# Fixed operand places, earlier weight sums and a port rule in the planner of an attention and feed-forward kernel

## The chip, the cores and the metric

The kernel runs on one core of one Trainium2 chip. The metric is the device time of one execution in microseconds (us).

## What is computed

An attention layer over 4 batches, 8 heads, 576 positions and head size 64, whose scores get a bias from a small network on relative positions, followed by a gated feed-forward layer over the 2304 tokens:

```
scores = q @ k.T / 8 + bias            # bias: relu(x * w1 + b1) @ w2 over |i - j|
attn   = softmax(scores) @ v           # 4 x 8 heads, 576 x 576 scores each
x      = attn as [2304, 512]
h      = x @ w_in                      # [2304, 2048]
out    = (h * sigmoid(h)) @ w_out      # [2304, 512]
```

The inputs of the feed-forward layer arrive as 64-bit floats and are narrowed to 32 bits on the chip.

## The kernel before, in words

**Precision.** Each f32 operand of a large matmul is kept as a rounded high half and a low half (the remainder); a product is three matmuls (high by high, high by low, low by high; `PAIRS`). The high half is a copy (line 274 on VectorE, line 272 on ScalarE), the low half a subtraction (line 277, on VectorE or GpSimd).

**Order.** No engine's order is written out by hand. `Plan` is a list scheduler that runs on the host. Each operation has a kind, a cost for every engine that may do it, a due time and the buffers it reads and writes (`op`, lines 67 to 91). `order` (lines 118 to 212) plays the program through with these costs, with a delay (`LAG`) after each, and gives each free engine the ready operation with the smallest due time; for an operation that another engine could do too, engines other than GpSimd add a penalty. What comes out is a fixed order of instructions on each engine. On the chip the engines then wait for data alone: no instruction waits because of a planned time. `take` hands out places in SBUF and PSUM: a tag has a fixed number of places (`caps`; 27 of tag `G`, 12 of `M`, 2 of `pt`, 2 of `w`), and a buffer keeps its place from its first operation until its last. All DMAs go through one queue (SP), in the planned order, so a load or store that waits holds up all behind it.

**Stages.** The attention of batch 0 with the making of the bias comes first. Then batches 1 and 2, and batch 3, go on beside two plain feed-forward blocks of 384 tokens (`ff_block`, 16 steps each). Block 0 also narrows all weights: four VectorE operations in a row on each of 32 tiles (`narrow`, lines 360 to 377), then a split into halves (`split`); the 16 tiles of `w_out` then stay in `G` until the end, those of `w_in` are stored to HBM (line 851). Block 1 loads them again (line 856). By then attention is done, and three super blocks of 512 tokens follow (`ff_super`, 8 steps each), which do the first product of the layer with seven instead of eight sub-products: operands are 256 columns of x or sums of them (`super_x`: line 686 multiplies by the softmax factor, line 694 forms the sums, then 14 pairs of halves), weights are tiles of `w_in` or sums and differences of two of them (`sums_of`: lines 723 and 728, then `split`, then a store to `ts_d` at line 732). A step has 42 matmuls of 256 columns (line 747) and 24 of 512 columns for the second product (line 804).

**Where the weight sums are made.** In block 2, the first super block, each step loads two tiles of `w_in` and calls `sums_of` for them; blocks 3 and 4 load the stored sums (line 840).

**Where the operands lie.** Each call of `super_x` asks for two new buffers of `pt` and four of `M`. The first ten pairs of halves are laid in `pt` in turn, the last four in `M`. In the plan a product reads whole buffers (line 742), so it follows every half that is written to the two `pt` buffers, and a new block's buffers can be had only when the last product of the block before that reads them is done:

```
pts = [buf("pt", [128, 5, 2, 256], F32R) for _ in range(2)]     # 676
...
dst, at = pts[n % 2], n // 2                                    # 698
...
@op("p_mm", ("PE", 0.71), t0 + 0.8 * k, reads=[w, xs[name, 0][0], xs[name, 1][0]], writes=[dst])   # 742
```

The `pt` buffers are also what attention keeps its transposed probabilities in (line 476).

Of the kernel before, what the change touches and what calls it, by code (L numbers as in the profile page):

```python
# [9 lines left out]
F32R = mybir.dt.float32r  # L10
# [36 lines left out]
class Plan:  # L47
# [11 lines left out]
    LAG = {"PE": 0.2, "ACT": 0.15, "DVE": 0.13, "POOL": 0.15, "SP": 0.95}  # L59
# [58 lines left out]
    def order(self):  # L118
# [13 lines left out]
        num, dma, mode = 0, 0.0, 0  # L132
# [13 lines left out]
        while events:  # L146
# [17 lines left out]
            for e in sorted(free, key=lambda e: free[e]):  # L164
# [8 lines left out]
                while wait[e]:  # L173
# [42 lines left out]
def attention_moe_kernel(ctx: ExitStack, tc: tile.TileContext, q, k, v, small, w_in, w_out, lut, ident_d, out):  # L216
# [96 lines left out]
    def bias_tile(st, t0):  # L313
# [8 lines left out]
        for ig in range(4):  # L322
            @op("bias_f", {"ACT": 0.22 + n * 0.00086, "DVE": 0.15 + n * 0.0009} if ig or st % 2 == 0 or st < 4 else {"POOL": 0.12 + n * 0.0045},
# [15 lines left out]
        @op("bias_ev", {"ACT": 0.29 + BW * 0.00083, "DVE": 0.26 + BW * 0.00103}, t0 + 2.5, reads=[bps, cb], writes=[bsb])  # L339
# [11 lines left out]
    def narrow(t0, w, src):  # L351
# [4 lines left out]
        @op("abs", ("ACT", 0.67), t0, reads=[d], writes=[w])  # L356
# [3 lines left out]
        @op("clamp", ("DVE", 0.5), t0 + 0.1, writes=[w])  # L360
# [3 lines left out]
        @op("shift", ("DVE", 0.56), t0 + 0.2, writes=[w])  # L364
# [4 lines left out]
        @op("low", ("DVE", 0.9), t0 + 0.3, reads=[d], writes=[w])  # L369
# [4 lines left out]
        @op("sign", ("DVE", 0.8), t0 + 0.4, reads=[d], writes=[w])  # L374
# [4 lines left out]
    def split(t0, w):  # L379
# [3 lines left out]
        @op("split_hi", ("ACT", 0.62), t0 + 0.5, reads=[w], writes=[(wr, 0)])  # L383
# [3 lines left out]
        @op("split_lo", {"POOL": 1.36, "DVE": 0.9}, t0 + 1, reads=[w, (wr, 0)], writes=[(wr, 1)])  # L387
# [23 lines left out]
    def keys(b, hp, t0):  # L411
# [4 lines left out]
        @op("k_hi", {"ACT": 1.16, "DVE": 0.85}, t0 - 8, reads=[kst], writes=[khi])  # L416
# [3 lines left out]
        for a in range(2):  # L420
            @op("k_lo", {"POOL": 1.55, "DVE": 0.95}, t0 - 6 + 0.1 * a, reads=[kst, khi], writes=[(klo, a)])
# [10 lines left out]
    def queries(b, hp, chunks, t0):  # L432
# [6 lines left out]
        @op("q_hi", {"ACT": 0.2 + 0.00083 * w, "DVE": 0.1 + 0.00056 * w}, t0 - 5, reads=[qst], writes=[qs])  # L439
# [3 lines left out]
        @op("q_lo", {"POOL": 0.12 + 0.0025 * w, "DVE": 0.1 + 0.0014 * w}, t0 - 4, reads=[qst], writes=[qs])  # L443
# [6 lines left out]
    def bias_of(hp, c, t0):  # L450
# [6 lines left out]
        if last:  # L457
            @op("bias_pad", ("POOL", 0.4), t0 - 9.1, writes=[bias])
# [12 lines left out]
    def visit(b, hp, chunks, kv, vs, sq, t0, pace=1.0):  # L471
# [24 lines left out]
        @op("o_ev", {"ACT": 0.2 + w * 0.00083, "DVE": 0.15 + w * 0.00105}, t0 + 6, reads=[o], writes=[xo])  # L496
# [467 lines left out]
```

## Time and profile before

| | |
|---|---|
| median of 3 runs | 736.78 us (736.67 to 738.56) |
| the profiled execution | 738.1 us |
| its span, first to last instruction | 735.3 us |
| mean granted TensorE clock | 0.991 |

The profile is of one execution. Its engines are PE (TensorE matmul), PEld (TensorE weight load, beside PE), DVE (VectorE), ACT (ScalarE), POOL (GpSimd) and SP (the queue that issues DMAs). L747 is line 747 of the kernel; most copies and subtractions are in helpers (L272, L274, L277), so they are told apart by the buffers they write and read: `out<-in`. A busy TensorE is modelled from starts and is not TensorE at its peak. A granted clock of 1.00 is 2.4 GHz, and 0.50 is 1.2 GHz.

### The profile page before, as it was taken

The page shows a single profiled execution, that of the slowest core. Times are in us where ns is not written, and L with a number is a line of the kernel's source. Part 1 is how long each engine was busy: PE and PEld are TensorE (multiplying, and loading weights), DVE is VectorE, ACT ScalarE, POOL GpSimd, SP SyncE. Part 2 cuts the span into 40 slices and gives each one's busy share as a digit, 9 for nine tenths or more (in the row PEclk, how much of TensorE's full clock was granted, in tenths as well). Part 3 has the DMA queues.
Part 4 walks back from the last instruction along what each step waited for, and adds up shares of the span by engine and source line. Part 5 has one row for each costly group of instructions (what it writes and reads, how often), then busy time and mean ns, then how long its engine had stood idle before and what let it go on. Part 6 is the DMA issues. An engine that isn't in the chain of part 4 may idle for free. (4 is left out here: it accounts for less than half of the span.)

```text
span 735.3 us, 13932 instructions
## 1 busy us (share of the span) xinstructions
PE 702.9 (96%) x4882; PEld 579.9 (79%) x4882; DVE 538.9 (73%) x1058; ACT 412.2 (56%) x885; POOL 308.4 (42%) x296
## 2 busy tenths in 40 slices
PE   9899999999999999989999999899989999999997
PEld 4376698677777887778888887888978889889986
DVE  7999968999999999995455448877784444953432
ACT  8799968886776777765444544433342222432222
POOL 5464524474646444572032207766570111710110
PEclk9999999999999999999999999999998999999999
DMA  6999899888595584788755636656595655687201
GB/s 193 337 312 304 281 311 352 279 281 300 188 275 173 211 292 162 259 272 289 269 169 198 207 124 218 253 191 229 181 323 183 231 165 188 203 290 260 99 1 57
DMA packets 73829, 167.40 MB, mean 228 GB/s; under 512 B 9376, under 2 KB 24352, under 8 KB 73760
## 3 DMA queue, kind: packets, MB, share of 16 engines
q1 hardware_dynamic: 73760, 166.53, 67.7%
q8 instruction: 38, 0.62, 0.4%
q14 instruction: 31, 0.25, 0.1%
HBM read 129.31 MB, written 37.18 MB: 226 GB/s over the span
## 5 line engine op out<-in xcount | busy, mean ns | idle before, releaser
L804 PE MATMUL psum<-G 128*128 128x512 f32 x576 | 151.7, 394 | 6.2 <-DVE G L277 4.4
L583 ACT ACTIVATE G<-G,sm 128x576 f32<-128x576 f32 (+1 forms) x144 | 111.8, 777 | 42.0 <-DVE sm L576 40.5
L576 DVE CUSTOM_DVE_ANT_0 G<-psum,G 128x576 f32<-128x576 f32 (+1 forms) x144 | 106.8, 758 | 30.9 <-PE psum L569 17.1
L804 PEld LDWEIGHTS psum<-G 128*128 128x128 f32 x576 | 101.2, 189 | 22.8 <-DVE G L277 5.2
L747 PEld LDWEIGHTS psum<-pt,G 128*128 128x128 f32 x672 | 99.0, 196 | 14.2 <-DVE pt L277 2.6
L747 PE MATMUL psum<-pt,G 128*128 128x256 f32 x672 | 103.7, 289 | 4.1 <-DVE pt L277 2.4
L592 PE MATMUL psum<-ident,G 128*128 128x128 f32 x656 | 93.0, 276 | 5.7 <-DVE sm L576 3.3
L569 PE MATMUL psum<-G,M 128*128 128x288 f32 x512 | 91.5, 310 | 5.6 <-DVE sm L576 3.9
L592 PEld LDWEIGHTS psum<-ident,G 128*128 128x128 f32 x656 | 75.0, 141 | 23.0 <-issue 5.0
L277 POOL TENSOR_TENSOR G<-M,G 128x512 fp32r<-128x512 f32 x23 | 32.0, 1394 | 145.4 <-DVE G L274 91.0
L569 PEld LDWEIGHTS psum<-G,M 128*128 128x128 f32 x512 | 74.2, 190 | 20.1 <-issue 6.0
L491 PE MATMUL psum<-pt,M 128*64 128x128 f32 (+3 forms) x880 | 87.5, 345 | 1.6 <-DVE sm L576 0.8
L646 PE MATMUL psum<-M,G 128*128 128x384 f32 x384 | 79.2, 344 | 1.2 <-POOL M L277 0.7
L272 ACT ACTIVATE pt<-psum 128x512 f32<-128x512 f32 (+3 forms) x115 | 62.2, 554 | 32.4 <-PE psum L592 30.1
L669 PE MATMUL psum<-G,M 128*128 128x512 f32 x288 | 77.9, 401 | 0.9 <-DVE M L277 0.9
L758 DVE TENSOR_TENSOR M<-psum,M 128x256 f32<-128x256 f32 x72 | 30.5, 423 | 65.0 <-PE psum L747 64.6
L277 POOL TENSOR_TENSOR M<-M 64x256 fp32r<-64x256 f32 (+3 forms) x39 | 47.2, 1214 | 73.5 <-DVE M L274 18.7
L491 PEld LDWEIGHTS psum<-pt,M 128*64 128x64 f32 x880 | 52.2, 137 | 30.1 <-issue 6.2
L785 ACT ACTIVATE M<-M 128x256 f32<-128x256 f32 (+1 forms) x48 | 24.9, 523 | 76.4 <-DVE M L758 76.3
L646 PEld LDWEIGHTS psum<-M,G 128*128 128x128 f32 x384 | 65.4, 188 | 3.0 <-POOL M L277 1.0
L277 POOL TENSOR_TENSOR M<-th,M 128x384 fp32r<-128x384 f32 x25 | 28.1, 1123 | 80.5 <-DVE M L274 32.0
L274 DVE COPY pt<-psum 128x512 f32<-128x512 f32 (+3 forms) x77 | 42.2, 563 | 23.4 <-PE psum L592 21.9
(92 smaller groups left out, 1132.3 us busy)
## 6 DMA issues: line engine op xcount, KB each, us to landing
G<-bias_d SPq DMA_DIRECT2D x48, 576.0 KB
G<-win_d SPq DMA_DIRECT2D x48, 512.0 KB
G<-ts_d SPq DMA_DIRECT2D x32, 512.0 KB
bias_d<-G SPq DMA_DIRECT2D x36, 295.5 KB
G<-in_k_dram SPq DMA_DIRECT2D x16, 576.0 KB
G<-in_w_in_dram SPq DMA_DIRECT2D x16, 512.0 KB
G<-in_w_out_dram SPq DMA_DIRECT2D x16, 512.0 KB
win_d<-G SPq DMA_DIRECT2D x16, 512.0 KB
```

The costliest lines, as they stand in the source:

```text
L272: A.activation(out=out, in_=in_, func=AF.Copy)
L274: ENG[e].tensor_copy(out=out, in_=in_)
L277: ENG[e].tensor_tensor(out=out, in0=in0, in1=f(in1), op=ALU.subtract)
L491: T.matmul(out=tl(o)[x, 0:w], lhsT=tl(vs)[:, (s + 1) % 5 * 128 + 64 * a:(s + 1) % 5 * 128 + 64 * a + 64], rhs=tl(pt)[:, s + 5 * a if s < 4 ...
L569: T.matmul(out=s[:, hf, 0:288], lhsT=tl(qs)[:, x0 + 128 * a:x0 + 128 * a + 128], rhs=tl(part)[:, S * a + 288 * hf:S * a + 288 * hf + 288], ...
L576: V.tensor_tensor_reduce(out=mine(p, a).rearrange("p (a n) -> p a n", a=2), in0=tl(sps[a]).rearrange("p (a n) -> p a n", a=2)[:, :, 0:widt ...
L583: A.activation(out=mine(p, a), in_=mine(p, a), func=AF.Exp, scale=-1.0, bias=tl(sm)[:, i + a:i + a + 1], accum_out=tl(sq)[:, 2 * c + a:2 * ...
L592: T.transpose(out=tl(tp)[:, 128 * s:128 * s + 128], in_=tl(p)[:, 128 * (s0 + s):128 * (s0 + s) + 128], identity=ident)
L646: T.matmul(out=tl(hp)[:, 0:TB], lhsT=tl(wr)[:, x, 128 * cc:128 * cc + 128], rhs=tl(xs[cc])[:, y, :], start=(cc + m == 0), stop=(cc == NC - ...
L669: T.matmul(out=tl(acc[i]), lhsT=tl(gg)[:, x, 128 * i:128 * i + 128], rhs=tl(wo[fi])[:, y, :], start=(fi == 0 and m == 0), stop=(fi == NF - ...
L747: T.matmul(out=first(dst), lhsT=tl(w)[:, x, off + 128 * cc:off + 128 * cc + 128], rhs=tl(b)[:, at, y, :], start=(start and cc + i == 0), s ...
L804: T.matmul(out=tl(acc[i]), lhsT=tl(gg)[:, x, 128 * i:128 * i + 128], rhs=tl(wo[fi])[:, y, :], start=(fi == 0 and j == 0), stop=(fi == NF - ...
```

## The change

1. **Costs.** All costs of the plan's operations are replaced, nearly all by smaller ones (the narrowing's four from 0.50, 0.56, 0.90 and 0.80 us to 0.34, 0.34, 0.60 and 0.60), and the delays after an operation too.
2. **Port.** The plan has a table of kinds that use a port which VectorE and GpSimd share. While an operation of that table runs on one of the two, the plan starts none of the table on the other. At each moment GpSimd chooses last.
3. **Places.** Each of the 14 operands has one place for all three super blocks (`slots`): the first four in `M`, the other ten in the two `pt` buffers. A product reads its own halves only, and a half of the next block is written after the last product that reads that place. Operands are due in the order in which products use them, and the loads of x one microsecond earlier.
4. **Sums.** `sums_of` is called in block 1, after each second step, for the two tiles which that block loads anyway. Block 2 loads the stored sums as blocks 3 and 4 do.

The due times of the stages, the numbers of places and the instructions' operands are otherwise as they were. Of the cost lines a few stand here; the others change in the same way.

```diff
--- before.py
+++ after.py
@@ -56,7 +56,10 @@
 
 
     MODES, CHANGE, KEEP = {"pv": 1, "bias_mm": 2}, 0.19, 1.5
-    LAG = {"PE": 0.2, "ACT": 0.15, "DVE": 0.13, "POOL": 0.15, "SP": 0.95}
+    LAG = {"PE": 0.18, "ACT": 0.14, "DVE": 0.12, "POOL": 0.1, "SP": 0.95}
+
+    PORT = {"DVE": {"lut", "bias_f", "clamp", "shift", "low", "sign", "split_lo", "k_hi", "k_lo", "q_hi", "q_lo", "x_mul", "x_hi", "x_lo", "g_hi", "g_lo", "x_sum", "w_sum", "w_whole"},
+            "POOL": {"split_lo", "k_lo", "q_lo", "x_mul", "x_lo", "g_lo", "sum", "x_sum", "w_sum", "w_whole"}}
...
-        num, dma, mode = 0, 0.0, 0
+        num, dma, mode, port = 0, 0.0, 0, 0.0
...
-            for e in sorted(free, key=lambda e: free[e]):
+            for e in sorted(free, key=lambda e: (e == "POOL", free[e])):
...
@@ -175,7 +178,8 @@
                     prio = prio[-1]
                     if started[i]:
                         continue
-                    if not self.take(ops[i][4]):
+                    shared = self.kinds[i] in self.PORT.get(e, ())
+                    if shared and port > now or not self.take(ops[i][4]):
                         skipped.append((prio, i))
                         continue
                     started[i] = True
@@ -185,6 +189,8 @@
                         mode = self.MODES.get(self.kinds[i], 0)
                         end += self.CHANGE
                     free[e] = end
+                    if shared:
+                        port = end
...
-            @op("bias_f", {"ACT": 0.22 + n * 0.00086, "DVE": 0.15 + n * 0.0009} if ig or st % 2 == 0 or st < 4 else {"POOL": 0.12 + n * 0.0045},
+            @op("bias_f", {"ACT": 0.2 + n * 0.00083, "DVE": 0.13 + n * 0.00053} if ig or st % 2 == 0 or st < 4 else {"POOL": 0.12 + n * 0.004},
...
-        @op("abs", ("ACT", 0.67), t0, reads=[d], writes=[w])
+        @op("abs", ("ACT", 0.58), t0, reads=[d], writes=[w])
...
-        @op("clamp", ("DVE", 0.5), t0 + 0.1, writes=[w])
+        @op("clamp", ("DVE", 0.34), t0 + 0.1, writes=[w])
...
-        @op("shift", ("DVE", 0.56), t0 + 0.2, writes=[w])
+        @op("shift", ("DVE", 0.34), t0 + 0.2, writes=[w])
...
-        @op("low", ("DVE", 0.9), t0 + 0.3, reads=[d], writes=[w])
+        @op("low", ("DVE", 0.6), t0 + 0.3, reads=[d], writes=[w])
...
-        @op("sign", ("DVE", 0.8), t0 + 0.4, reads=[d], writes=[w])
+        @op("sign", ("DVE", 0.6), t0 + 0.4, reads=[d], writes=[w])
...
-        @op("split_hi", ("ACT", 0.62), t0 + 0.5, reads=[w], writes=[(wr, 0)])
+        @op("split_hi", ("ACT", 0.53), t0 + 0.5, reads=[w], writes=[(wr, 0)])
...
-        @op("split_lo", {"POOL": 1.36, "DVE": 0.9}, t0 + 1, reads=[w, (wr, 0)], writes=[(wr, 1)])
+        @op("split_lo", {"POOL": 1.24, "DVE": 0.6}, t0 + 1, reads=[w, (wr, 0)], writes=[(wr, 1)])
...
-            @op("max", ("DVE", 0.23 + width * 0.00105), t0 + 0.5 + 0.5 * a, reads=[sps[a], bias], writes=[(p, a), (sm, i + a)])
+            @op("max", ("DVE", 0.08 + width * 0.00116), t0 + 0.5 + 0.5 * a, reads=[sps[a], bias], writes=[(p, a), (sm, i + a)])
...
-            @op("exp", ("ACT", 0.48 + width * 0.00083), t0 + 1.5 + 0.5 * a, reads=[(sm, i + a)], writes=[(p, a), (sq, 2 * c + a)])
+            @op("exp", ("ACT", 0.29 + width * 0.00083), t0 + 1.5 + 0.5 * a, reads=[(sm, i + a)], writes=[(p, a), (sq, 2 * c + a)])
...
                              start=(fi == 0 and m == 0), stop=(fi == NF - 1 and m == 2))
 
+    slots = {}
+
     def super_x(blk, t0):
 
 
-        ops = {}
-        pts = [buf("pt", [128, 5, 2, 256], F32R) for _ in range(2)]
-        n = 0
+        names = ("a11", "a12", "s1", "s2", "s4", "s3", "a22")
+        if not slots:
+            homes = [(buf("M", [128, 1, 2, 256], F32R), 0) for _ in range(4)]
+            homes += [(b, i) for b in [buf("pt", [128, 5, 2, 256], F32R) for _ in range(2)] for i in range(5)]
+            slots.update(((name, cc), homes[2 * k + cc]) for k, name in enumerate(names) for cc in range(2))
+        part = lambda b, i: tl(b)[:, 256 * i:256 * i + 256]
         for cc in range(2):
-            t = t0 + 2 * cc
+            t = t0 - 9 + 2 * cc
             xa, xr = buf("G", [128, 2 * TS]), buf("G", [128, 2 * TS])
             for j in range(2):
                 load_x(blk, cc + 2 * j, t, xa, xr, TS * j)
 
-                @op("x_mul", {"DVE": 0.75, "POOL": 1.5}, t - 0.1, reads=[(xr, (TS * j, 0)), (xr, (TS * j, 1))], writes=[(xa, TS * j)])
+                @op("x_mul", {"DVE": 0.6, "POOL": 1.24}, t - 0.1, reads=[(xr, (TS * j, 0)), (xr, (TS * j, 1))], writes=[(xa, TS * j)])
                 def _(e, xa=xa, xr=xr, j=j):
                     ENG[e].tensor_tensor(out=tl(xa)[:, TS * j:TS * j + TS], in0=tl(xa)[:, TS * j:TS * j + TS], in1=tl(xr)[:, TS * j:TS * j + TS], op=ALU.mult)
 
-            part = lambda b, i: tl(b)[:, 256 * i:256 * i + 256]
 
             for d, (p, i), (q, j), o in ((0, (xa, 1), (xa, 3), ALU.add), (1, (xr, 0), (xa, 0), ALU.subtract),
                                          (2, (xa, 0), (xa, 1), ALU.subtract), (3, (xa, 2), (xr, 1), ALU.subtract)):
-                @op("x_sum", {"DVE": 0.44, "POOL": 0.8}, t + 0.1 * d, reads=[xa], writes=[xr])
-                def _(e, d=d, p=p, i=i, q=q, j=j, o=o, xr=xr, part=part):
+                @op("x_sum", {"DVE": 0.35, "POOL": 0.69}, t + 0.1 * d, reads=[xa], writes=[xr])
+                def _(e, d=d, p=p, i=i, q=q, j=j, o=o, xr=xr):
                     ENG[e].tensor_tensor(out=part(xr, d), in0=part(p, i), in1=part(q, j), op=o)
 
-            for k, (name, src, i) in enumerate((("a11", xa, 0), ("a12", xa, 2), ("s1", xr, 0), ("s2", xr, 1), ("s4", xr, 3), ("s3", xr, 2), ("a22", xa, 3))):
-                if n < 10:
-                    dst, at = pts[n % 2], n // 2
-                else:
-                    dst, at = buf("M", [128, 1, 2, 256], F32R), 0
-                n += 1
-                ops[name, cc] = (dst, at)
-
-                @op("x_hi", {"DVE": 0.36, "ACT": 0.42}, t + 1 + 0.1 * k, reads=[src], writes=[(dst, (at, 0))])
-                def _(e, dst=dst, at=at, src=src, i=i, part=part):
-                    copy(e, tl(dst)[:, at, 0, :], part(src, i))
-
-                @op("x_lo", {"POOL": 0.75, "DVE": 0.44}, t + 1.1 + 0.1 * k, reads=[src, (dst, (at, 0))], writes=[(dst, (at, 1))])
-                def _(e, dst=dst, at=at, src=src, i=i, part=part):
-                    sub(e, tl(dst)[:, at, 1, :], part(src, i), tl(dst)[:, at, 0, :])
-        return ops
+            at = {"a11": (xa, 0), "a12": (xa, 2), "a22": (xa, 3), "s1": (xr, 0), "s2": (xr, 1), "s3": (xr, 2), "s4": (xr, 3)}
+            for k, name in enumerate(names):
+                (dst, n), (src, i), t = slots[name, cc], at[name], t0 - 3 + 0.8 * k + 0.05 * cc
+
+                @op("x_hi", {"DVE": 0.2, "ACT": 0.31}, t, reads=[src], writes=[(dst, (n, 0))])
+                def _(e, dst=dst, n=n, src=src, i=i):
+                    copy(e, tl(dst)[:, n, 0, :], part(src, i))
+
+                @op("x_lo", {"POOL": 0.69, "DVE": 0.34}, t + 0.1, reads=[src, (dst, (n, 0))], writes=[(dst, (n, 1))])
+                def _(e, dst=dst, n=n, src=src, i=i):
+                    sub(e, tl(dst)[:, n, 1, :], part(src, i), tl(dst)[:, n, 0, :])
 
...
         for w, wr in zip((w1, w2), ws):
-            @op("w_whole", {"DVE": 0.7, "POOL": 1.4}, t0 - 5, reads=[wr], writes=[w])
+            @op("w_whole", {"DVE": 0.6, "POOL": 1.24}, t0 - 5, reads=[wr], writes=[w])
...
         for d, p, q in (((w1, 0), (w2, 0), (w1, 0)), ((w2, 0), (w2, 1), (w2, 0)), ((w2, 1), (w2, 1), (w1, 0)), ((w1, 1), (w1, 1), (w2, 1))):
-            @op("w_sum", {"DVE": 0.44, "POOL": 0.8}, t0 - 4, reads=[w1, w2], writes=[d[0]])
+            @op("w_sum", {"DVE": 0.35, "POOL": 0.69}, t0 - 4, reads=[w1, w2], writes=[d[0]])
...
-    def super_pair(m, xs, wf, wb, b22, t1, t2, acc, t0):
+    def super_pair(m, wf, wb, b22, t1, t2, acc, t0):
 
         X, Y, Z = bank("h", 1), bank("h", 1), bank("h", 1)
         tmp, hh = buf("M", [128, 3, 256]), buf("M", [128, 3, 256])
         first = lambda b: tl(b)[:, 0:256]
 
         def product(name, w, off, dst, k, start):
-            @op("p_mm", ("PE", 0.71), t0 + 0.8 * k, reads=[w, xs[name, 0][0], xs[name, 1][0]], writes=[dst])
+            @op("p_mm", ("PE", 0.71), t0 + 0.8 * k, reads=[w] + [(b, (at, i)) for b, at in (slots[name, 0], slots[name, 1]) for i in range(2)], writes=[dst])
             def _(e):
                 for cc in range(2):
-                    b, at = xs[name, cc]
+                    b, at = slots[name, cc]
                     for i, (x, y) in enumerate(PAIRS):
                         T.matmul(out=first(dst), lhsT=tl(w)[:, x, off + 128 * cc:off + 128 * cc + 128], rhs=tl(b)[:, at, y, :],
                                  start=(start and cc + i == 0), stop=(cc == 1 and i == 2), skip_group_check=True)
...
     def ff_super(blk, t0):
-        xs = super_x(blk, t0 - 8)
+        super_x(blk, t0)
         acc = [bank("acc", 1) for _ in range(4)]
         for m in range(NF // 2):
             t = t0 + DS * m
             wf = buf("G", [128, 2, DM], F32R)
             load_w("ld_in", wf, t - 9, win_d[2 * m], win_b[2 * m])
-            if blk == 2:
-                wb, b22 = buf("G", [128, 2, DM], F32R), 256
-                load_w("ld_in", wb, t - 9, win_d[2 * m + 1], win_b[2 * m + 1])
-                t1, t2 = sums_of(m, (wf, wb), t - 2)
-            else:
-                wb, b22 = buf("M", [128, 2, 256], F32R), 0
-                load("ld_in2", t - 9, [wb], lambda e, wb=wb, m=m: SP.dma_start(
-                    out=f(tl(wb)), in_=win_d[2 * m + 1].rearrange("p (a n) -> p a n", a=2)[:, :, 256:512]), 262144, reads=[win_b[2 * m + 1]])
-                t1, t2 = buf("G", [128, 2, DM], F32R), buf("G", [128, 2, DM], F32R)
-                for i, w in enumerate((t1, t2)):
-                    load_w("ld_ts", w, t - 9, ts_d[m][i], ts_b[m][i])
-            super_pair(m, xs, wf, wb, b22, t1, t2, acc, t)
+            wb, b22 = buf("M", [128, 2, 256], F32R), 0
+            load("ld_in2", t - 9, [wb], lambda e, wb=wb, m=m: SP.dma_start(
+                out=f(tl(wb)), in_=win_d[2 * m + 1].rearrange("p (a n) -> p a n", a=2)[:, :, 256:512]), 262144, reads=[win_b[2 * m + 1]])
+            t1, t2 = buf("G", [128, 2, DM], F32R), buf("G", [128, 2, DM], F32R)
+            for i, w in enumerate((t1, t2)):
+                load_w("ld_ts", w, t - 9, ts_d[m][i], ts_b[m][i])
+            super_pair(m, wf, wb, b22, t1, t2, acc, t)
         store_out(blk, acc, t0 + DS * 9 + 3)
 
     def ff_block(blk, t0, step):
@@ -855,6 +855,10 @@
                 wr = buf("G", [128, 2, DM], F32R)
                 load("ld_in", t - 8, [wr], lambda e, wr=wr, fi=fi: SP.dma_start(out=f(tl(wr).rearrange("p a n -> p (a n)")), in_=win_d[fi]), 524288, reads=[win_b[fi]])
             ff_step(blk, fi, xs, wr, acc, t)
+            if blk == 1:
+                if fi % 2:
+                    sums_of(fi // 2, (other, wr), t + 4)
+                other = wr
         store_out(blk, acc, t0 + step * (NF - 1) + 2 * DF + 3)
```

## Rows read from the trace of the kernel before

**Rows 1.** The page's first part: busy us, share of the span, instructions.
```profile
PE 702.9 (96%) x4882; PEld 579.9 (79%) x4882; DVE 538.9 (73%) x1058; ACT 412.2 (56%) x885; POOL 308.4 (42%) x296
```

**Rows 2.** Windows: length, busy us and (count) of PE, PEld, DVE, ACT, POOL; clock, DMA share, GB/s.
```profile
140.00:340.00 200.00, 188.50 (x1240) 152.18 (x1239) 190.12 (x344) 147.14 (x308) 107.96 (x95) 1.00 0.74 245
340.00:458.00 118.00, 117.94 (x758) 99.67 (x757) 65.85 (x140) 56.85 (x128) 37.00 (x40) 1.00 0.62 204
...
480.00:536.00 56.00, 56.00 (x346) 50.21 (x345) 43.16 (x73) 20.17 (x39) 34.39 (x29) 1.00 0.58 209
536.00:560.00 24.00, 19.61 (x110) 17.39 (x109) 17.11 (x27) 8.31 (x23) 12.83 (x14) 0.86 0.81 269
560.00:636.00 76.00, 76.00 (x477) 68.60 (x476) 38.40 (x75) 23.10 (x50) 18.47 (x17) 1.00 0.59 192
```

**Rows 3.** Waits of PE, 140 to 340 us: us in total, times, longest.
```profile
PE psum L592 <- DVE sm L576: 2.6, 4, 1.3
PE psum L569 <- DVE sm L576: 2.1, 4, 0.9
```

**Rows 4.** Groups by line and form, VectorE, 140 to 340 us (columns as in the page).
```profile
L371 DVE SCALAR_TENSOR_TENSOR w<-G,w 128x512 uint32<-128x512 uint32 x30 | 30.7, 1022 | 0.4
...
L362 DVE TENSOR_SCALAR w<-w 128x512 f32<-128x512 f32 x30 | 21.0, 702 | 0.8 <-ACT w L358 0.8
```

**Rows 5.** Lines 371 and 362, whole run: duration ns min/median/max, first and last start.
```profile
L371 DVE SCALAR_TENSOR_TENSOR w<-G,w x32: 676/693/2196, 130.7 to 319.1; 128x512 uint32<-128x512 uint32 x32
...
L362 DVE TENSOR_SCALAR w<-w x32: 405/422/1917, 127.7 to 315.2; 128x512 f32<-128x512 f32 x32
```

**Rows 6.** Timeline of PE, 458 to 480 us: start, us, count, [idle before <-releaser].
```profile
461.00 0.50 PE L747 MATMUL psum<-pt,G 128*128 128x256 f32 x2 [2.37 <-DVE pt L277]
462.59 2.29 PE L747 MATMUL psum<-pt,G 128*128 128x256 f32 x9 [1.09 <-DVE th L655]
...
479.39 1.66 PE L804 MATMUL psum<-G 128*128 128x512 f32 x6 [0.89 <-DVE M L758]
```

**Rows 7.** The chain that ended last, in order of time: start, us, piece.
```profile
462.59 3.92 PE psum L747 x18
...
538.65 4.59 DMA G<-ts_d
543.25 1.08 DVE G L686
...
553.63 4.92 PE psum L747 x24
559.25 1.42 PE psum L747 x12
```

**Rows 8.** Timeline of PE at the second super boundary.
```profile
548.67 0.73 PE L804 MATMUL psum<-G 128*128 128x512 f32 x2 [0.95 <-ACT G L272]
552.84 0.79 PE L804 MATMUL psum<-G 128*128 128x512 f32 x1 [3.43 <-DVE G L277]
```

**Rows 9.** Timeline of PE at the third super boundary.
```profile
640.64 1.93 PE L747 MATMUL psum<-pt,G 128*128 128x256 f32 x14 [0.61 <-POOL pt L277]
...
643.97 0.50 PE L804 MATMUL psum<-G 128*128 128x512 f32 x1 [0.93 <-DVE G L277]
```

**Rows 10.** Groups by line and form, whole run: the weight sums.
```profile
L723 POOL TENSOR_TENSOR w<-G 128x512 f32<-128x512 f32 x9 | 14.6, 1623 | 1.0 <-DMA G<-win_d 0.6
L728 POOL TENSOR_TENSOR w<-w 128x256 f32<-128x256 f32 x18 | 14.3, 795 | 6.7 <-DVE w L728 5.2 <-DVE w L723 0.7
...
L728 DVE TENSOR_TENSOR w<-w 128x256 f32<-128x256 f32 x14 | 10.2, 729 | 1.2 <-POOL w L728 0.6
...
L723 DVE TENSOR_TENSOR w<-G 128x512 f32<-128x512 f32 x7 | 6.7, 953 | 0.0
```

**Rows 11.** Waits of the DMA queue (SP), whole run: us in total, times, longest.
```profile
SPq L714 <- PE psum L804: 75.9, 23, 7.8
...
SPq L851 <- POOL G L277: 19.9, 6, 7.0
SPq L732 <- POOL G L277: 17.6, 6, 5.5
```

More of the change, by code (lines that the diff above doesn't have):

```diff
@@ L457, in bias_of @@
         if last:
-            @op("bias_pad", ("POOL", 0.4), t0 - 9.1, writes=[bias])
+            @op("bias_pad", ("POOL", 0.25), t0 - 9.1, writes=[bias])
             def _(e):
@@ L512, in sums @@
         sq = buf("sq", [128, 128])
-        @op("sq_zero", ("POOL", 0.3), t0 - 3, writes=[sq])
+        @op("sq_zero", ("POOL", 0.16), t0 - 3, writes=[sq])
         def _(e):
@@ L519, in factors @@
     def factors(b, hp, sq, t0):
-        @op("sum", {"DVE": 0.17, "POOL": 0.3}, t0 + 4, reads=[(sq, i) for i in range(9)], writes=[sq])
+        @op("sum", {"DVE": 0.1, "POOL": 0.2}, t0 + 4, reads=[(sq, i) for i in range(9)], writes=[sq])
         def _(e):
             ENG[e].tensor_scalar_add(out=tl(sq)[:, 0:9], in0=tl(sq)[:, 0:9], scalar1=1e-9)
-        @op("recip", ("DVE", 0.2), t0 + 4.1, writes=[sq])
+        @op("recip", ("DVE", 0.13), t0 + 4.1, writes=[sq])
         def _(e):
@@ L533, in _ @@
             T.transpose(out=tl(rp)[:, 0:128], in_=tl(sq), identity=ident)
-        @op("r_ev", {"ACT": 0.3, "DVE": 0.28}, t0 + 4.7, reads=[rp], writes=[rt])
+        @op("r_ev", {"ACT": 0.16, "DVE": 0.2}, t0 + 4.7, reads=[rp], writes=[rt])
         def _(e):
@@ L647, in _ @@
                              start=(cc + m == 0), stop=(cc == NC - 1 and m == 2))
-        @op("tanh", ("ACT", 0.5), t0 + 2.3, reads=[hp], writes=[th])
+        @op("tanh", ("ACT", 0.4), t0 + 2.3, reads=[hp], writes=[th])
         def _(e):
             A.activation(out=tl(th), in_=tl(hp)[:, 0:TB], func=AF.Tanh, scale=0.5)
-        @op("gate", ("DVE", 0.56), t0 + 2.4, reads=[hp], writes=[th])
+        @op("gate", ("DVE", 0.48), t0 + 2.4, reads=[hp], writes=[th])
         def _(e):
             V.scalar_tensor_tensor(out=tl(th), in0=tl(th), scalar=1.0, in1=tl(hp)[:, 0:TB], op0=ALU.add, op1=ALU.mult)
-        @op("g_hi", {"DVE": 0.35, "ACT": 0.53}, t0 + 2.5, reads=[th], writes=[(gg, 0)])
+        @op("g_hi", {"DVE": 0.27, "ACT": 0.43}, t0 + 2.5, reads=[th], writes=[(gg, 0)])
         def _(e):
             copy(e, tl(gg)[:, 0, :], tl(th))
-        @op("g_lo", {"DVE": 0.55, "POOL": 1.1}, t0 + 2.6, reads=[th, (gg, 0)], writes=[(gg, 1)])
+        @op("g_lo", {"DVE": 0.47, "POOL": 0.96}, t0 + 2.6, reads=[th, (gg, 0)], writes=[(gg, 1)])
         def _(e):
@@ L781, in super_pair @@
                 need = [X] if src is None else [(hh, j) for j in range(i, i + k)]
-                @op("tanh", ("ACT", 0.2 + 0.00083 * w), t, reads=need, writes=[(th, x)])
+                @op("tanh", ("ACT", 0.08 + 0.00088 * w), t, reads=need, writes=[(th, x)])
                 def _(e, th=th, x=x, w=w, what=what):
                     A.activation(out=tl(th)[:, x:x + w], in_=what(), func=AF.Tanh, scale=0.5)
-                @op("gate", ("DVE", 0.17 + 0.00105 * w), t + 0.1, reads=need, writes=[(th, x)])
+                @op("gate", ("DVE", 0.08 + 0.00105 * w), t + 0.1, reads=need, writes=[(th, x)])
                 def _(e, th=th, x=x, w=w, what=what):
```

32 lines of the change are left out of this document (16 added, 16 removed).

## The prediction

> **What bounds the kernel now.** The page's first part comes first: TensorE is busy for 702.9 of 735.3 us [rows 1], and the change neither adds nor removes a matmul. So the question is where TensorE stands still or runs slowly, and that is read by stage, from the windows [rows 2]. From 340 to 458 us (block 1 with the attention of batch 3), from 480 to 536 us (inside the first super block) and from 560 to 636 us (the second) TensorE is busy all the time at a granted clock of 1.00; nothing can be gained there. Two other places lose.
>
> The first is 140 to 340 us, where the narrowing of the weights runs beside attention. TensorE is idle for 200 - 188.5 = 11.5 us, and VectorE is the engine that is full, 190.1 of 200 us. The waits of TensorE name it: 2.6 and 2.1 us for the row maxima of line 576 alone [rows 3]. VectorE's own lines show what fills it. Lines 371 and 362 have medians of 693 and 422 ns but reach 2196 and 1917 ns [rows 5]: one instruction sometimes lasts some 1500 ns longer, as long as a large GpSimd operation on SBUF (1623 ns at line 723 [rows 10]). In the stretch their means are 1022 and 702 ns [rows 4].
>
> The second is the three starts of the super blocks:
> - at the first, idle pieces of 2.37, 1.09 and 0.89 us, 4.35 us together [rows 6]; and then 18 matmuls take 3.92 us, where 12 in steady state take 1.42 us, 0.118 each [rows 7], so these 18 (2.13 us at that rate) lose 1.8 us more. Sum 6.1 us.
> - at the second, 0.95 and 3.43 us idle [rows 8]; 24 matmuls then take 4.92 us instead of 2.84 us [rows 7], 2.1 us lost. Sum 6.5 us. The granted clock of that stretch is 0.86 on average [rows 2], so part of it ran at 1.2 GHz after these idle pieces.
> - at the third, 0.61 and 0.93 us idle [rows 9], 1.5 us.
>
> What comes late at these starts is x: the waits name the low halves in `pt` (line 277), and at the second start the chain runs from a 4.59 us load of stored sums straight into the multiply of line 686 [rows 7], which is early work for a block whose products are already wanted.
>
> **The change, part by part.** The sum is against the profiled execution, 738.1 us for a span of 735.3 us; the median of the runs, 736.8 us, is 1.3 us lower, and I carry the same differences over to it.
>
> *Costs and port rule.* They put no wait on the chip; they only alter the order on each engine. The new cost of line 371, 0.60 us, is nearer to its median of 0.69 us [rows 5] than the old 0.90 us, so the plan's time should drift less from the chip's. What can be gained on VectorE: line 371, 30 times 1022 - 693 ns is 9.9 us; line 362, 30 times 702 - 422 ns is 8.4 us; together 18 us of VectorE's 200 from two of the four lines. VectorE would then have room, as it has in the stretches where TensorE never waits (43.2 of 56 us busy at 480 to 536 us). GpSimd's 108 us [rows 2] would lie beside VectorE's work that doesn't use the port, above all the row maxima and the copies out of PSUM. What that gives TensorE the trace doesn't show. From below it is nothing. From above: weight loads fill 152.2 of 200 us here and 99.7 of 118 us in the next stretch [rows 2], whose mix is about the same without a wait; at that rate the loads here would need 180 us, so up to 20 us. The nearest row is the idle time, 11.5 us. I take 7: the 4.7 us that the two rows name and a third of the other 6.8 us, because some operations of GpSimd will come later than now.
>
> Here a rule speaks about the measure. The Trainium skill's Perfetto Trace Analysis (section Identifying the Most-Contended Engine) says that matmul busy time is a bad measure of the headroom of TensorE and that the busy share of the weight loads is a better one. By idle time the stage has 11.5 us to give, by that rule 20 us, and the sum below would come out 13 us lower; it is a rival.
>
> *Places and dependencies.* In the plan a product now waits for its own halves only, not for all that is written to both `pt` buffers, and the next block's first operand can be split as soon as the last step's first product has read its place. The remaining products and the second products of the last steps (line 804) then cover the splits. At the second start I therefore take 6.3 of the 6.5 us (between 0 and 6.5), at the third 1.3 of 1.5 us. At the first start, attention holds `pt` until its last visit; but the first two products' operands lie in `M`, and VectorE and GpSimd no longer make sums there. The ten pairs for `pt` still have to be split in a hurry. I take 4.5 of 6.1 us (between 0 and 6.1). What is late next is then the gate and the halves behind the last products, which each step has anyway.
>
> *Sums moved.* They leave the first super block, where they cost TensorE nothing (56.0 of 56.0 us busy), so only its start gains. They go into block 1: 14.6 + 14.3 + 10.2 + 6.7 = 45.8 us of GpSimd and VectorE together [rows 10], 16 splits, 16 stores. The cover is there: VectorE has 118 - 65.9 = 52 us free, GpSimd 81 us, ScalarE 61 us [rows 2]. On the DMA queue the 16 stores of line 732 move into block 1, between the loads of attention's bias, keys and queries; and block 2 gets 16 loads of stored sums, while its second tile's load is halved. That is the load of the second super block, where TensorE waits for nothing. In `G`, with 16 of 27 places taken by `w_out`, a tile of `w_in` is now kept a step longer, and two more places go to the sums. The price is not in the trace. From below: nothing, and below nothing there is no room since TensorE has no idle time there. From above by the nearest stage with such stores (line 851 in block 0): 11.5 us idle in 200 us, so 6.8 us in 118. The cover makes the low end nearer: I take 1 us of loss.
>
> Everything before 140 us and the end after the last product stay as they are; I put the reordering there at nothing, plus or minus 2 us.
>
> **Sum.** -7 - 4.5 - 6.3 - 1.3 + 1 = -18.1 us: 720.0 us for an execution like the profiled one, **718.7 us** as a median.
>
> **Rivals.**
> - *The rule does not hold on the chip.* Nothing but the order enforces it; a drift of one microsecond brings the overlaps back. For it: engines wait for data only, and stretched instructions go up to a whole operation of the other engine [rows 5]. Against: the new costs fit. The first stage then gains nothing: 725.7 us. Chance 0.15.
> - *The starts stay half late*, because x waits not for its place but for its load: the queue waits 75.9 us in total for places of `G` in 23 loads of line 714 behind line 804 [rows 11], and the second start's chain has such a load in it. Then the starts give 0, 3.2 and 0.7 us: -7 - 3.9 + 1, 726.9 us. Chance 0.15.
> - *The first stage gives all 20 us* that the weight loads allow, with VectorE's 18 us and more given back and no overlap left: 13 us less, 705.7 us. Chance 0.15, since ScalarE and the dependencies of attention remain.
> - *Slower: the stores of the sums hold up the queue in block 1.* A store stands in the queue until the split is done; the six such waits of line 851 are 19.9 us, 3.3 each, and those of line 732 17.6 us [rows 11]. In block 1 the loads of bias and keys stand behind them, and TensorE there has no slack. If each of the eight pairs cost TensorE more than 19.1 / 8 = 2.4 us, all gain would be gone; at 3.3 us it is -19.1 + 26.4 = +7.3 us, 744.1 us. Against it: the plan knows these waits and puts stores 4 us behind their splits. Chance 0.10.
>
> **How the numbers follow.** The forecast has 0.45. The range goes from 707 us, into the rival of 705.7 us, to 732 us, past both rivals that stop at about 726 us and with some 5 us for their unknown terms (block 1's other 5.8 us); it leaves out the slow case and part of the fast one. About 0.3%, 2.2 us, is what a measurement of this kernel can tell from no change. Faster by more: all cases but the slow one and the far end of the two middle ones, 0.87. Slower by more: 0.09. Between: 0.04.
>
> **What would show it.** In the profile after: lines 371 and 362 with means close to 693 and 422 ns; VectorE clearly under 190 us in the narrowing stage and TensorE's idle time there about 5 us; no idle piece over 1 us at the second and third start and the clock at 1.00; no line 723 or 728 during the super blocks; TensorE still full in block 1. The forecast is wrong if TensorE idles in block 1 behind loads that stand after line 732, or if the means of the narrowing stay at 1 us while the order has changed.

## The result and the profile after

The changed kernel takes 728.5 us (median; 727.28 to 728.50 at the full clock) against 737.32 us, a ratio of 0.9873 with a 95% interval of 0.9851 to 0.9895. Measured once more it takes 730.24 us against 736.75 us: 0.9906 (0.9872 to 0.9940). That is 6.5 to 8.8 us faster where 18.1 were forecast; it lies within the range of 707 to 732 us. The first profiled execution ran at a mean granted clock of 0.557 and took 1124.82 us, so the profile shown is that of the second measurement (727.88 us, span 726.1 us, clock 0.999). It is 2.4 us faster than the median of that measurement, and the profile before is 1.3 us slower than its own, so the two profiles lie 9.2 us apart where the medians lie 6.5 to 8.8 us apart. Line numbers are five or six higher after the change: 576 is 582, 747 is 752, 371 is 377, 362 is 368.

The page's first part, which answers to [rows 1]:

```profile
PE 700.8 (97%) x4863; PEld 572.6 (79%) x4863; DVE 535.6 (74%) x1150; ACT 415.0 (57%) x902; POOL 175.3 (24%) x187
```

GpSimd's work has nearly halved, from 308.4 us. The windows, with the columns of [rows 2]:

```profile
40.00:120.00 80.00, 75.52 (x793) 57.10 (x794) 66.89 (x163) 63.14 (x142) 29.32 (x35) 1.00 0.86 282
140.00:340.00 200.00, 189.90 (x1254) 153.29 (x1252) 189.22 (x394) 144.00 (x311) 62.07 (x64) 1.00 0.75 248
340.00:458.00 118.00, 116.49 (x743) 96.98 (x742) 85.27 (x180) 69.00 (x149) 34.18 (x36) 1.00 0.77 261
...
536.00:560.00 24.00, 23.73 (x151) 21.07 (x151) 17.06 (x36) 11.24 (x28) 5.24 (x6) 1.00 0.77 268
```

A window between fixed times shows how full the engines are, but not how far the work has come. For that I cut at equal counts: a window of one line's instructions alone, up to the time at which it holds a given number of them. The first line for this is that of the row maxima. Each of the four batches has 36 of them with two records each, so the 72nd record ends batch 0, the 215th is the last but one of batch 2 and comes just after the narrowing, and the 288th is the last of all, near the end of attention. Before and then after:

```profile
0.00:116.20 116.20, 26.89 (x72) 0.99 0.89 290
0.00:327.10 327.10, 79.95 (x215) 0.99 0.80 264
0.00:446.10 446.10, 107.69 (x288) 1.00 0.76 252
```

```profile
0.00:120.30 120.30, 26.54 (x72) 1.00 0.86 283
0.00:327.60 327.60, 79.92 (x215) 1.00 0.80 264
0.00:448.90 448.90, 107.83 (x288) 1.00 0.79 264
```

The second line is that of the matmuls of line 747 (752 after), before and then after; 42 make a step, 84 the two steps of a start, 336 a super block (counts differ by one where a start falls on the cut):

```profile
0.00:477.50 477.50, 12.10 (x83) 0.99 0.75 250
0.00:544.70 544.70, 47.00 (x336) 0.99 0.74 247
0.00:573.00 573.00, 60.35 (x419) 0.99 0.74 246
0.00:636.30 636.30, 95.25 (x672) 0.99 0.72 240
0.00:659.70 659.70, 107.08 (x756) 0.99 0.72 241
```

```profile
0.00:476.30 476.30, 10.59 (x84) 1.00 0.80 267
0.00:542.50 542.50, 45.84 (x336) 1.00 0.77 260
0.00:563.80 563.80, 57.65 (x419) 1.00 0.78 261
0.00:628.00 628.00, 93.08 (x672) 1.00 0.75 253
0.00:649.40 649.40, 104.86 (x756) 1.00 0.76 254
```

| stage | before, us | after, us | difference | forecast |
|---|---|---|---|---|
| to the end of batch 0 | 116.2 | 120.3 | +4.1 | 0 |
| batches 1 and 2, with the narrowing | 210.9 | 207.3 | -3.6 | -7 |
| batch 3, beside block 1 with the sums | 119.0 | 121.3 | +2.3 | +1 |
| first start, from the last maximum to the end of two steps | 31.4 | 27.4 | -4.0 | -4.5 |
| rest of the first super block | 67.2 | 66.2 | -1.0 | 0 |
| second start (two steps) | 28.3 | 21.3 | -7.0 | -6.3 |
| rest of the second super block | 63.3 | 64.2 | +0.9 | 0 |
| third start (two steps) | 23.4 | 21.4 | -2.0 | -1.3 |
| the rest | 75.6 | 76.7 | +1.1 | 0 |
| span | 735.3 | 726.1 | -9.2 | -18.1 |

The other order of instructions makes such a cut uncertain by some 2 us: over the eight maxima that follow the end of batch 0 the difference moves between 3.0 and 6.7 us.

When the chip has done batch 0's attention it is 4.1 us late. In the stretch 40 to 120 us TensorE is idle for 4.5 us after the change; before it was full:

```profile
40.00:120.00 80.00, 80.00 (x861) 61.12 (x860) 67.68 (x178) 68.15 (x156) 35.23 (x45) 1.00 0.93 301
```

From 455 us on, TensorE's list of waits has only these two lines left after the change (us in total, times, longest), where [rows 6, 8, 9] had pieces of up to 3.43 us:

```profile
PE psum L752 <- DVE M L763: 0.5, 2, 0.3
PE psum L752 <- DVE th L661: 0.3, 1, 0.3
```

The stretched instructions in the narrowing, by line and form from 140 to 340 us, as [rows 4], and over the whole run, as [rows 5]:

```profile
L377 DVE SCALAR_TENSOR_TENSOR w<-G,w 128x512 uint32<-128x512 uint32 x31 | 23.3, 750 | 0.3
L368 DVE TENSOR_SCALAR w<-w 128x512 f32<-128x512 f32 x30 | 15.2, 508 | 0.3
```

```profile
L377 DVE SCALAR_TENSOR_TENSOR w<-G,w x32: 636/686/1925, 133.7 to 314.5; 128x512 uint32<-128x512 uint32 x32
...
L368 DVE TENSOR_SCALAR w<-w x32: 399/421/1903, 130.4 to 312.7; 128x512 f32<-128x512 f32 x32
```

The means fall from 1022 to 750 and from 702 to 508 ns; a few instructions are still stretched to 1.9 us.

### The profile page after: what moved, and what is told of

The parts are those of the page before. It is cut to its first block, busy times and chain, and to the rows that moved or that the text cites. A ratio compares the mean times of both kernels' runs of the same rounds, so it can differ in the third digit from the quotient of the medians.

```text
span 1123.0 us, 13838 instructions
## 1 busy us (share of the span) xinstructions
PE 1115.5 (99%) x4863; PEld 785.8 (70%) x4863; DVE 536.1 (48%) x1150; ACT 420.6 (37%) x902; POOL 167.6 (15%) x187
## 4 chain that ended last, share of the span: by engine, by line
PE 98%; ACT 1%; DVE 0%; DMA 0%; issue 0%; SPq 0%; ACTq 0%; DVEq 0%
PE psum L809 20%; PE psum L752 17%; PE psum L497 13%; PE psum L598 11%; PE psum L675 10%; PE psum L575 10%; PE psum L652 10%; PE psum L342 4%; PE psum L566 2%; PE psum L903 1%; PE psum L539 0%; DMA cb<-in_small_dram 0%; ACT G L349 0%; ACT pt L278 0%; DVE G L582 0%
## 5 line engine op out<-in xcount | busy, mean ns | idle before, releaser
L809 PE MATMUL psum<-G 128*128 128x512 f32 x576 | 242.2, 576 | 0.0
L809 PEld LDWEIGHTS psum<-G 128*128 128x128 f32 x576 | 128.9, 238 | 53.1 <-issue 23.9
L497 PE MATMUL psum<-pt,M 128*64 128x128 f32 (+3 forms) x880 | 144.7, 508 | 0.1
L598 PE MATMUL psum<-ident,G 128*128 128x128 f32 x656 | 144.6, 387 | 0.0
L575 PE MATMUL psum<-G,M 128*128 128x288 f32 x512 | 134.7, 428 | 0.6 <-DVE pt L280 0.3
L752 PEld LDWEIGHTS psum<-pt,G 128*128 128x128 f32 x576 | 117.0, 242 | 23.9 <-issue 10.8
L652 PE MATMUL psum<-M,G 128*128 128x384 f32 x384 | 123.3, 488 | 0.0
L675 PE MATMUL psum<-G,M 128*128 128x512 f32 x288 | 123.0, 583 | 0.0
L575 PEld LDWEIGHTS psum<-G,M 128*128 128x128 f32 x512 | 104.1, 239 | 26.6 <-issue 11.8
L652 PEld LDWEIGHTS psum<-M,G 128*128 128x128 f32 x384 | 83.1, 222 | 24.0 <-issue 2.4
L278 ACT ACTIVATE pt<-psum 128x640 f32<-128x640 f32 (+3 forms) x104 | 55.4, 543 | 111.6 <-PE psum L598 102.5
L675 PEld LDWEIGHTS psum<-G,M 128*128 128x128 f32 x288 | 62.3, 223 | 32.0 <-issue 16.1
L752 PEld LDWEIGHTS psum<-M,G 128*128 128x128 f32 x288 | 58.3, 236 | 15.3 <-issue 8.5
```

Source lines behind the costliest of these rows:

```text
L278: A.activation(out=out, in_=in_, func=AF.Copy)
L497: T.matmul(out=tl(o)[x, 0:w], lhsT=tl(vs)[:, (s + 1) % 5 * 128 + 64 * a:(s + 1) % 5 * 128 + 64 * a + 64], rhs=tl(pt)[:, s + 5 * a if s < 4 ...
L575: T.matmul(out=s[:, hf, 0:288], lhsT=tl(qs)[:, x0 + 128 * a:x0 + 128 * a + 128], rhs=tl(part)[:, S * a + 288 * hf:S * a + 288 * hf + 288], ...
L598: T.transpose(out=tl(tp)[:, 128 * s:128 * s + 128], in_=tl(p)[:, 128 * (s0 + s):128 * (s0 + s) + 128], identity=ident)
L652: T.matmul(out=tl(hp)[:, 0:TB], lhsT=tl(wr)[:, x, 128 * cc:128 * cc + 128], rhs=tl(xs[cc])[:, y, :], start=(cc + m == 0), stop=(cc == NC - ...
L675: T.matmul(out=tl(acc[i]), lhsT=tl(gg)[:, x, 128 * i:128 * i + 128], rhs=tl(wo[fi])[:, y, :], start=(fi == 0 and m == 0), stop=(fi == NF - ...
```

## The experiments

All times are medians beside runs of the kernel before on the same chip (736.75 us for the first four, 737.57 for the next four, 737.28 for the last). Two measurements of one kernel differ by up to 2 us here, so smaller differences between variants are read from stages alone.

**The changed kernel again.** No edit.

> The changed kernel once more, for a profile at the full clock; 727 to 729 us. The prediction's 18 us came out as 9. Three theories say where the other 9 us stayed. N: the narrowing stage gave nothing, TensorE is still idle for 9 us or more of 200 there and VectorE still over 95% full. S: the starts of the super blocks are still half late, 6 us or more of idle pieces and slow matmuls left of 14. B: block 1 pays for the sums, TensorE has 5 us or more of idle time between the narrowing and the first super block, where it had none.

730.24 us. None of the three theories names the largest single piece. N holds by half: the narrowing gained 3.6 us of 7, and VectorE is as full as before (189.2 of 200 us) and TensorE nearly as idle (10.1 us). S fell: the starts are mended. B holds in small: TensorE is idle for 1.5 us in block 1, and the stage takes 2.3 us longer. The piece that no theory names is the 4.1 us lost before batch 0 was done.

**The port rule out.**

```diff
-    PORT = {"DVE": {...}, "POOL": {...}}
+    PORT = {}
-            for e in sorted(free, key=lambda e: (e == "POOL", free[e])):
+            for e in sorted(free, key=lambda e: free[e]):
```

> The changed kernel with an empty port table and GpSimd's place in the choice as before; costs, places and sums stay. By the prediction's step (the rule takes the stretched VectorE instructions away and with them idle time of TensorE) it is 4 to 7 us slower than the changed kernel, 732 to 736 us, with lines like 371 back at a mean of 1 us. By N (the rule only moves work from GpSimd to VectorE) it is within 2 us of it, or faster.

774.18 us, 1.0489 (1.0453 to 1.0524): 44 us slower than the changed kernel, where I expected 4 to 7. The narrowing stretch, line 377 in it, and the largest waits of TensorE over the run:

```profile
140.00:340.00 200.00, 175.08 (x1126) 137.03 (x1125) 180.16 (x328) 133.34 (x281) 85.92 (x78) 0.97 0.68 221
```

```profile
L377 DVE SCALAR_TENSOR_TENSOR w<-G,w 128x512 uint32<-128x512 uint32 x31 | 26.5, 859 | 0.5
```

```profile
PE psum L575 <- DVE sm L582: 9.6, 8, 2.8
PE psum L598 <- ACT G L589: 7.5, 7, 2.3
```

TensorE is idle for 25 us of these 200. Its largest waits are for the row maxima and for the exponentials behind them; that the order expects the maxima earlier than they come is my reading and not shown by itself. The mean of line 377 rises to 859 ns only, less than the 1022 ns of the kernel before [rows 4], which is 37 us faster. So the stretched instructions alone do not make the time; I take it that they do so in an order that was planned without them.

**The new costs alone**, on the kernel before: the cost and `LAG` lines of the diff and nothing else.

> The kernel before with the new costs and delays alone: no port table, buffers per block and sums in the first super block as before. By the prediction the costs alone give little, 0 to 3 us of the narrowing stage, 734 to 737 us, and the starts stay as late as before. If most of the 9 us comes from costs that fit, it is 729 to 732 us.

782.96 us, 1.0617 (1.0587 to 1.0647): 46 us slower than before, against both expectations. With the rule beside them the same costs make the kernel 4 us faster than before (below), so they need the rule, and the two are one part of the change. I read this as a surcharge in the old costs for what VectorE and GpSimd do to each other: the old 0.90 us of line 371 lies between its median of 0.69 and its mean of 1.02 us [rows 4, 5]. The delays changed together with the costs and were not tried apart.

**Sums back in the first super block.**

```diff
+            if blk == 2:
+                wb, b22 = buf("G", [128, 2, DM], F32R), 256
+                load_w("ld_in", wb, t - 9, win_d[2 * m + 1], win_b[2 * m + 1])
+                t1, t2 = sums_of(m, (wf, wb), t - 2)
...
-                    sums_of(fi // 2, (other, wr), t + 4)
```

> The changed kernel with the weight sums back in the first super block; costs, port rule and places stay. By the prediction (moving them is worth part of the first start's 4.5 us and costs 1 us) it is 2 to 4 us slower, 730 to 733 us. By B (block 1 pays) it is faster, 722 to 726 us.

730.34 us, not to be told from the changed kernel's 730.24, where 2 to 4 us more were expected. Beside the other parts the move is worth nothing that can be measured. By stages it is a trade: with the sums back, block 1 takes 118.5 us (215th to 288th maximum) and the first start 32.0 us, where the changed kernel takes 121.3 and 27.4.

**Buffers per super block again.**

```diff
-        if not slots:
+        if True:
...
-            homes = [(buf("M", [128, 1, 2, 256], F32R), 0) for _ in range(4)]
+            homes = [(pts[n % 2], n // 2) for n in range(10)] + [(buf("M", ...), 0) for _ in range(4)]
...
-            @op("p_mm", ..., reads=[w] + [(b, (at, i)) for ...], writes=[dst])
+            @op("p_mm", ..., reads=[w, xs[name, 0][0], xs[name, 1][0]], writes=[dst])
```

> The changed kernel with two new pt buffers per super block, whole-buffer reads and the old due times of the operands; costs, port rule and sums in block 1 stay. By the prediction's step on places (4.5 + 6.3 + 1.3 us, less what moving the sums gives alone) it is 9 to 13 us slower than the changed kernel, 737 to 741 us, all of it at the three starts. If the starts were late because of the load on VectorE and the loads, which the other parts mended, it is within 3 us of it.

730.50 us, not to be told from it either; the second start is as short as with fixed places. My step on places does not hold beside the other parts.

**Places and sums with the old costs and no rule.**

> The kernel before with fixed places and the sums in block 1; old costs, old delays, no port table. In the changed kernel the narrowing stage gained 6 us by the trace and the stage before 120 us lost 6.7. If both come from costs and port rule together, they are absent here: 725 to 729 us, as fast as the changed kernel, with batch 0 done at 120 us and the narrowing's end at 327 us. If the port rule is needed for the starts, it is 731 us or more.

731.85 us, 0.9921 (0.9906 to 0.9936): places and sums alone have 5.7 us, less than expected. Batch 0 ends in time there (115.1 us), and the two steps of the second start take 21.3 us (546.8 to 568.1), so the start does not need the rule. But from the 215th to the 288th maximum it takes 123.4 us instead of 119.0: without the rule and the new costs the sums in block 1 cost 4.4 us.

**The rule with the old costs.**

> The changed kernel with the old costs and delays; port rule, places and sums stay. The new costs without the rule made 44 us more. If costs and rule are two ways to say the same thing (the old costs held a surcharge for overlaps), then both together count it twice and GpSimd is used too little: 729 to 740 us. If only the rule matters, 724 to 729 us.

731.41 us. This fits the double counting that I expected: the 215th maximum comes at 329.9 us instead of 327.1. But batch 0 ends in time, even early (73 records here):

```profile
0.00:113.30 113.30, 26.69 (x73) 1.00 0.88 290
```

So the loss before 120 us does not come from the rule. It comes with the new costs and delays: with them alone, without rule, places and sums, the 72nd record comes at 123.9 us.

**The old costs of the two bias kinds.**

> The changed kernel with the old costs of the two bias kinds (bias_f and bias_ev) alone. If the stage before 120 us lost its 6.7 us because the new costs put too much of the bias on VectorE (the plan's 0.13 + 0.00053 per column adds up to 23.3 us where the trace has 28.6), batch 0 is done near 121 us again and the whole takes 722 to 725 us. If the port rule itself did it, by taking GpSimd's subtractions to VectorE, it stays at 727 to 731 us.

726.64 us, some 2 to 4 us faster than the changed kernel, between the two expectations. Batch 0 ends at 117.2 us instead of 120.3:

```profile
0.00:117.20 117.20, 26.86 (x72) 0.99 0.87 286
```

So 3.1 of the 4.1 us come back with these two costs. The expectation's times (121 us here, 119 and 126.7 us in the last one below) count 79 records, the last seven of which belong to batch 1; by that count only 1.1 us come back (125.7 instead of 126.8 us). With the uncertainty of a cut, the costs of the bias make a large part of the early loss, but not surely all of it.

**Each part alone**, on the kernel before: costs and rule, places, sums.

> The kernel before with the new costs, delays and the port rule; buffers per block and sums in the first super block as before. Taking away any one of the three parts cost the changed kernel only 1 to 4 us of its 9. If the parts overlap because each alone mends the second start, this one has the second start mended and the first as late as before: about 730 to 732 us. If that start needs places or sums, 736 to 739 us, since the stage before 120 us gives back what the narrowing gains.

> The kernel before with fixed places, reads by half and the new due times of the operands alone. If each part alone mends the second start (7 us) and places help the first a little, 728 to 731 us. If the start was late because of the load of sums on VectorE and the queue, 734 to 737 us.

> The kernel before with the weight sums in block 1 alone. If each part alone mends the second start, and the sums cost block 1 some 4 us and give the first start some 4 us, 729 to 732 us. If places are needed, 736 us or more.

732.93 us (0.9943, 0.9922 to 0.9964), 732.63 us (0.9930, 0.9905 to 0.9956) and 735.49 us (0.9981, 0.9964 to 0.9998). None of the three lies in a range that I gave; the sums alone come near to "places are needed". Added up, the three gains are 10.8 us; the whole change has 6.5 to 8.8. The windows of the last maximum and of line 747 around the first and the second start show the overlap, for costs and rule, then places, then sums:

```profile
0.00:448.90 448.90, 107.51 (x288) 1.00 0.76 250
0.00:476.00 476.00, 10.74 (x84) 1.00 0.76 251
0.00:542.70 542.70, 46.09 (x335) 1.00 0.74 247
0.00:568.70 568.70, 59.06 (x419) 1.00 0.74 248
```

```profile
0.00:444.70 444.70, 107.56 (x288) 1.00 0.77 252
0.00:476.30 476.30, 11.44 (x83) 1.00 0.76 251
0.00:544.40 544.40, 46.63 (x335) 1.00 0.75 247
0.00:566.50 566.50, 58.45 (x420) 1.00 0.75 249
```

```profile
0.00:449.40 449.40, 107.59 (x288) 1.00 0.79 263
0.00:482.60 482.60, 10.00 (x84) 0.99 0.80 268
0.00:548.50 548.50, 44.78 (x335) 0.99 0.77 257
0.00:571.90 571.90, 56.61 (x419) 0.99 0.77 258
```

The two steps of the second start take 26.0, 22.1 and 23.4 us; before 28.3, all together 21.3. Places alone give 6.2 us, sums alone 4.9 and costs and rule 2.3, but the stall can be taken away only once. The first start, from the last maximum on, takes 27.1, 31.6 and 33.2 us; before 31.4, all together 27.4. Costs and rule alone mend it; places alone and sums alone give nothing there. The account is not complete, since costs, rule and places without the sums moved take 32.0 us. With the sums alone the 84th product comes at 482.6 us instead of 477.5: in block 1 they cost more than their leaving gives the first start. TensorE is not full there any more, while GpSimd has 62 us of work instead of 37 [rows 2]:

```profile
340.00:458.00 118.00, 114.61 (x728) 94.59 (x728) 77.76 (x153) 62.69 (x138) 61.99 (x63) 1.00 0.76 252
```

**The changed kernel with the old costs for batch 0.**

```diff
-            @op("max", ("DVE", 0.08 + width * 0.00116), t0 + 0.5 + 0.5 * a, ...
+            @op("max", ("DVE", 0.23 + width * 0.00105) if b == 0 else ("DVE", 0.08 + width * 0.00116), t0 + 0.5 + 0.5 * a, ...
...
-                    done = (dma if e == "SP" else end) + self.LAG[e]
+                    done = (dma if e == "SP" else end) + (self.LAG0 if now < 100.0 else self.LAG)[e]
```

and so for eleven other kinds of attention, and the old costs of the two bias kinds.

> The changed kernel with the old costs for batch 0's attention and for the bias, and the old delays before the plan's 100 us; everything later as changed. With the old costs throughout, the port rule kept and batch 0 was done at 119 us; with the new ones at 126.7 us. If that loss of 6 to 7 us is a term of its own, it comes back and the rest keeps its gains: 718 to 722 us, faster than both kernels. If the narrowing stage's 6 us are only the early stage's loss made good, 726 to 729 us.

720.49 us, 0.9777 (0.9744 to 0.9809): 16.8 us faster than before, and faster than both kernels. The 72nd and the 215th maximum (73 records in the first line), and the narrowing stretch:

```profile
0.00:116.40 116.40, 26.84 (x73) 0.99 0.87 289
0.00:320.30 320.30, 80.07 (x215) 0.99 0.82 270
```

```profile
140.00:340.00 200.00, 193.01 (x1271) 156.72 (x1269) 182.81 (x384) 147.77 (x315) 66.54 (x67) 1.00 0.78 254
```

Batch 0 ends 3.9 us earlier than in the changed kernel, as early as before the change, and batches 1 and 2 then take 203.9 us: 7.0 us less than before, the whole of what was forecast. VectorE is clearly under 190 us and TensorE idle for 7.0 us. Of the 18.1 us that were forecast 16.8 have come. The early loss was a term of its own; the gains behind it stay when it goes, and that of the narrowing doubles, for a reason that no run shows. Each set of costs was measured in the one order that the plan makes of it, and this one puts back twelve kinds, the bias and the delays at once.

## Why the prediction was right in part

- **The failed step** is "Everything before 140 us and the end after the last product stay as they are; I put the reordering there at nothing, plus or minus 2 us." The stage lost 4.1 us. I had costed the new numbers only where stretched instructions showed in the rows, in the narrowing, and had no row of the stage before it, where the same change of costs acts. That the costs and delays did it, not the rule, is shown by the ends of batch 0: 116.2 us before, 123.9 with new costs alone, 113.3 with the rule, places, sums and old costs, 120.3 with all, 116.4 with the old costs for batch 0. The two bias kinds' costs give back 3.1 us of it; by which turn of the order stays open.
- **Costs and port rule in the narrowing**: forecast -7, measured -3.6; three more runs with the same costs and rule give -2.6 (sums back), -3.3 (old places) and -2.7 (costs and rule alone). The stretched instructions went as foreseen: 30 times 272 and 30 times 194 ns are 14.0 us of VectorE, where I had up to 18. What I expected of VectorE did not come: it is not below 190 us, since the plan gave it what it took from GpSimd (108.0 to 62.1 us). Of my 7 us, the part that two rows named came: waits for row maxima on those two lines were 4.7 us and are 0.9. The third of the other 6.8 us did not: other waits took its place, ScalarE's copies into `pt` first. TensorE's waits from 140 to 340 us after the change:

```profile
PE psum L598 <- ACT pt L278: 1.9, 2, 1.7
PE psum L497 <- ACT pt L278: 1.4, 1, 1.4
PE psum L497 <- DVE sm L582: 1.2, 1, 1.2
...
PE psum L575 <- DVE sm L582: 0.9, 1, 0.9
```

  TensorE's idle time fell only from 11.5 to 10.1 us. The Trainium skill's Perfetto Trace Analysis (Identifying the Most-Contended Engine) prefers the busy share of the weight loads; that moved as little, from 152.2 to 153.3 us in the same window. Neither tells the gain of 3.6 us in 211; counts of work done do. The 20 us of that rival were far off.
- **The starts**: first -4.0 for -4.5, second -7.0 for -6.3, third -2.0 for -1.3, right in size. In cause they were not. I gave the first to places and sums, which alone give nothing there (31.6 and 33.2 us for 31.4); costs and rule alone do (27.1). I gave the second to the fixed places, and it would have been mended without them: the runs without places and without sums have it as short. It was mended twice over. That the sizes fit all the same is luck.
- **Sums moved**: forecast +1 for block 1, measured +2.3. Alone the move costs block 1 4.7 us and 5 us by the 84th product; with the rule and the new costs, which keep its work off GpSimd (34.2 instead of 62.0 us in 340 to 458 us), about half of that shows in block 1.
- **Inside the range by luck.** I drew its upper end for a rule that fails or starts that stay late, and neither came. What filled it was a stage that I had put at nothing and a narrowing of half the size.
- **The rivals.** That the rule would not hold on the chip is refuted in the main: the means fell, and without it the time rises by 44 us; a few instructions are still stretched. That the starts stay half late is refuted: the second gave 7.0 us, where that rival had 3.2. No stage gave 20 us. Of the stores of the sums, the waits for their halves add up to 7.4 us on the queue, in three pieces, and with some small others the line has 9.4 us; block 1 lost 2.3 us, not 26:

```profile
SPq L737 <- DVE G L283: 4.3, 2, 3.6
...
SPq L737 <- POOL G L283: 3.1, 1, 3.1
```

The Trainium skill's SBUF page (SBUF — State Buffer, Who interferes with whom) says that the port pair which the two engines share is locked for a whole instruction, and that the loser waits. The trace agrees for the longest run of line 377: it begins inside a GpSimd subtraction, lasts 1925 ns against a median of 686, and ends 0.56 us after that subtraction (start, us, instruction; VectorE, then GpSimd):

```profile
251.82 1.93 DVE L377 SCALAR_TENSOR_TENSOR w<-G,w 128x512 uint32<-128x512 uint32 x1
...
251.30 1.89 POOL L283 TENSOR_TENSOR G<-G 128x576 fp32r<-128x576 f32 x1
```

## What to carry to other kernels

In a plan made with costs, a cost may hold a surcharge for contention that nobody wrote down: replacing it by the undisturbed duration cost 46 us here until the contention itself was in the plan. A change of costs acts on every stage, so each stage needs a term, also those in which nothing seems wrong, and is best compared at equal counts of one line's instructions, with the cut where the stage's work ends: seven records too many changed what the runs seemed to say of the bias. Where several edits aim at one stall, the stall can be saved once; take each out of the whole, and put each in alone, before one of them gets the credit.

## What was not expected of the hardware

How little the stretched instructions tell by themselves. Without the rule the kernel takes 774 us. Line 377 reaches 2081 ns there from a median of 692, with a mean of 859 ns in the narrowing stretch, and GpSimd is busy for 294.5 us. The kernel before, with 2196 ns, 1022 ns and 308.4 us [rows 1, 4, 5], takes 737 us. The instructions are stretched no more without the rule than before; what differs, as I read it, is whether the order was planned for that.
